# A decode step of attention and a gated MLP: the last row of weights in two pieces, a one-row store, and small loads in halves

## The chip, the cores and the metric

The kernel runs on one core of a Trainium2 chip. A time is device time in microseconds (us) of one execution, the median of several. Five engines work side by side: PE (TensorE, matmuls; its weight loads are listed as PEld), DVE (VectorE), ACT (ScalarE), POOL (GpSimd) and SP (SyncE, which here only issues transfers and waits). Data comes from HBM through 16 DMA engines that all queues share. SBUF and PSUM have 128 partitions; PSUM takes the results of PE.

## The reference

One token, D = 576. Two branches see the same x and are mixed by a gate:

```
g = sigmoid(sum(x * gate_w))
q = x @ wq                          # 32 heads of 128
k, v = last 4096 positions of the caches, 16 heads, each for 2 heads of q
a = softmax(q k^T / sqrt(128)) v @ wo          # wo: 4096 x 576
b = gelu(x @ w1 + b1) @ w2 + b2                # w1: 576 x 4608, w2: 4608 x 576
out = g * a + (1 - g) * b                      # 1 x 576, bfloat16
```

All inputs are bfloat16. About 54 MB are read once; the output has 1152 bytes.

## The kernel before

Large tensors are read in transfers of 128 partitions, all issued by SP: eight k_t and eight v_t of 2 MB each (two heads), two each of wq, w1 and wo, and w2 as four groups (NG = 4) of 1152 rows. In a group each partition holds nine whole rows of w2 (RJ = 9, 10,368 bytes). Group 2 comes in two transfers and the last group in three: rows 0 to 5, rows 6 and 7, and row 8 alone (L625 to L630). Small loads go through ACT's queue at the very start: x, gate_w and b_2, each as one row of 1152 bytes on one partition (L130 to L132). x comes a second time, spread over 64 partitions, through SP (x9, L136).

The order of work on each engine is the order written in the kernel (a manual schedule). The gate comes first: DVE multiplies x and gate_w and sums (L385), PE spreads the sum to all partitions (g_ps, L390), ACT and DVE make the sigmoid. Then, over pairs of heads, PE transposes keys (L235), ACT and DVE copy them out of PSUM (L246, L244), PE makes scores, softmax runs in blocks of four heads, and PE multiplies with the values. The MLP's first half runs between the heads. A load into a buffer waits until PE has done with what was in it.

At the end PE multiplies wo and the first three groups of w2 into the tile part, on four rows of PSUM (partitions 0, 32, 64, 96). DVE adds these to (1 - g) * b_2 (part_s, L679). Then `row_matmul` (L688) adds everything into y_ps: one row of 576 results is held as four quarters of DQ = 144 columns, on partitions 0, 32, 64 and 96 of one PSUM tile. For each of the nine rows j of the last group there are four matmuls, one a quarter. DVE casts y_ps to the SBUF tile y, all 128 partitions at once (L703), and SP stores four of its partitions, 288 bytes each, to the output (L704).

The framework puts in the waits. Its transfers take eight completion semaphores in turn. A transfer that takes a semaphore again is issued only when the one eight before it has landed. Behind the last instruction SP waits for all of them (these stand under L732, the end of the kernel), two to an instruction, in this order in the compiled program: (4th, 3rd), (5th, 2nd), (6th, 1st), (7th, DVE), (8th, ACT); then a barrier of all engines ends the program.

Of the kernel before, what the change touches and what calls it, by code (L numbers as in the profile page):

```python
# [9 lines left out]
BF16 = mybir.dt.bfloat16  # L10
# [6 lines left out]
def kernel(  # L17
# [15 lines left out]
    nc = tc.nc  # L33

    P = 128
    D = 576
# [10 lines left out]
    NQ = 4  # L47
    DQ = D // NQ

    RJ = 9  # L50
    NG = F // (P * RJ)
# [27 lines left out]
    const = ctx.enter_context(tc.tile_pool(name="const", bufs=1))  # L79
# [13 lines left out]
    w2_view = B_w2.rearrange("(g p j) n -> g p (j n)", p=P, j=RJ)  # L93
# [31 lines left out]
    x_row = const.tile([1, D], BF16, name="x_row")  # L125
    gw_row = const.tile([1, D], BF16, name="gw_row")

    b2_r = const.tile([P, D], BF16, name="b2_r")
    nc.gpsimd.memset(b2_r[:], 0.0)
    nc.scalar.dma_start(out=x_row[:], in_=A_x.rearrange("a b d -> (a b) d"))  # L130
    nc.scalar.dma_start(out=gw_row[:], in_=gate_w.rearrange("(o n) -> o n", o=1))
    nc.scalar.dma_start(out=b2_r[0:1, :], in_=B_b2.rearrange("(o n) -> o n", o=1))  # L132

    k_tiles[0] = load_k(0)
    x9 = const.tile([P // 2, NM], BF16, name="x9")
# [3 lines left out]
    for i in range(2):  # L139
# [16 lines left out]
        out=row_f[:], in_=ident_f[:, 0 : 32 * (NQ - 1) + 1 : 32], axis=AX.X, op=ALU.add  # L156
# [4 lines left out]
        out=dup[:].rearrange("k (i e) -> k i e", e=2),  # L161
        in_=ident[0 : P // 2, 0 : P // 2].rearrange("k (i e) -> k i e", e=1).to_broadcast(
            [P // 2, P // 2, 2]
        ),
    )
    par = const.tile([P, 2], FP32, name="par")
    for o in range(2):
        nc.vector.tensor_reduce(
            out=par[:, o : o + 1],
            in_=ident_f[:].rearrange("p (i o) -> p o i", o=2)[:, o, :],  # L170
# [7 lines left out]
        out=turn[:].rearrange("p j (h q) -> p j h q", h=OJ),  # L178
        in_=ident[:].rearrange("p (o q j) -> p j o q", o=1, j=OJ).to_broadcast(
            [P, OJ, OJ, P // OJ]  # L180
        ),
# [4 lines left out]
        out=m_r[:], in_=ident_f[:].rearrange("p (s r) -> p r s", r=R), axis=AX.X, op=ALU.add  # L186
# [5 lines left out]
        out=row_e[:], in_=ident_f[:].rearrange("p (a e q) -> p e a q", e=2, q=2), axis=AX.XY,  # L192
# [3 lines left out]
        out=row_e[:], in0=row_e[:], scalar1=-MASK, scalar2=MASK, op0=ALU.mult, op1=ALU.add  # L196
    )
    mask = const.tile([P, BC * P], BF16, name="mask")
    for e in range(2):
        nc.vector.tensor_copy(  # L200
            out=mask[:, e::2], in_=row_e[:, e : e + 1].to_broadcast([P, BC * P // 2])
# [4 lines left out]
        out=m_c[:], in_=ident_f[:].rearrange("p (t c r) -> p c t r", c=BC, r=R), axis=AX.XY,  # L206
# [4 lines left out]
        out=m_hl[:], in_=ident_f[:].rearrange("p (h q) -> p h q", h=OJ), axis=AX.X, op=ALU.add  # L211
# [10 lines left out]
    for dst, src in ((sel, ident), (sel_f, ident_f)):  # L222
        nc.vector.tensor_copy(
            out=dst[:].rearrange("p l (o h) -> p l o h", o=2),
            in_=src[:].rearrange("p (h l x) -> p l x h", h=2, l=2)[:, :, 0:2, :],
# [149 lines left out]
    for dst, src, s in (  # L375
# [10 lines left out]
        out=junk[:], in0=x_row[:], in1=gw_row[:], scale=1.0, scalar=0.0,  # L386
# [11 lines left out]
        out=omg[:], in0=g_t[:], scalar1=-1.0, scalar2=1.0, op0=ALU.mult, op1=ALU.add  # L398
# [7 lines left out]
    for b in range(NM * NQ):  # L406
        m, t = b // NQ, b % NQ
# [22 lines left out]
    for m in range(HB // 2):  # L430
        lo = R * (NGR - 1) + RP * m
        nc.vector.tensor_copy(  # L432
            out=qz[:, m :: HB // 2, lo : lo + RP],
            in_=qT[:, :, m, :].rearrange("p i b -> p b i"),
# [114 lines left out]
    for h in range(NU):  # L549
# [4 lines left out]
        if h == 1:  # L554

            for o in range(2):
                nc.sync.dma_start(
                    out=b1_r[o : o + 32 * (NQ - 1) + 1 : 32],
                    in_=B_b1.rearrange("(o t k n) -> o t k n", o=2, t=NQ, k=2)[o],
# [57 lines left out]
    for i in range(NOG // 2):  # L617
        t = w_pool.tile([P, WMAX], BF16, name="wo_t", tag="w")
        nc.sync.dma_start(
            out=t[:, 0 : 2 * OJ * D].rearrange("p (o n) -> p o n", o=2),  # L620
            in_=wo_view[:, 2 * i : 2 * i + 2, :],
# [2 lines left out]
    w2_t = []  # L624
    for g in range(NG):  # L625
        t = kv_pool.tile([P, NCK * Dh], BF16, name="w2_t", tag="kv")
        cut = {NG - 2: (0, 5, RJ), NG - 1: (0, 6, 8, RJ)}.get(g, (0, RJ))
        for lo, hi in zip(cut, cut[1:]):
            nc.sync.dma_start(out=t[:, lo * D : hi * D], in_=w2_view[g, :, lo * D : hi * D])
        w2_t.append(t)  # L630

    ot = const.tile([P, Hq], BF16, name="ot")
# [1 line left out]
        out=ot[:], in0=o_sb[:], scalar=g_t[:, 0:1], in1=r_sums[:], op0=ALU.mult, op1=ALU.mult  # L634
# [3 lines left out]
    for j in range(OJ):  # L638
# [3 lines left out]
        out=ow_m[:],  # L642
# [5 lines left out]
    with nc.allow_low_precision("one of the eight summands is not zero"):  # L648
        nc.vector.tensor_reduce(  # L649
            out=ow[:].rearrange("p j o -> p (j o)"), in_=ow_m[:], axis=AX.X, op=ALU.add  # L650
# [4 lines left out]
    y_ps = ps_s.tile([P, DQ], FP32, name="y_ps", tag="s")  # L655
# [12 lines left out]
    for n, four in enumerate(blocks):  # L668
# [11 lines left out]
        out=part_s[:], in0=b2_r[:].rearrange("p (k n) -> p k n", k=2), scalar=omg[:, 0:1],  # L680
# [5 lines left out]
    quarters = [slice(t * DQ, (t + 1) * DQ) for t in range(NQ)]  # L686
# [10 lines left out]
    for j in range(RJ):  # L697
# [1 line left out]
        row_matmul(  # L699
            gt[:, j, NG - 1 : NG], [row[:, q] for q in quarters], False, j == RJ - 1  # L700
        )
    y = const.tile([P, DQ], BF16, name="y")
    nc.vector.tensor_copy(out=y[:], in_=y_ps[:])  # L703
    nc.sync.dma_start(  # L704
        out=out.rearrange("a b (t n) -> (a b t) n", t=NQ), in_=y[0 : 32 * (NQ - 1) + 1 : 32, :]
    )


# [28 lines left out]
```

## Time and profile before

| what | value |
|---|---|
| median of 3 runs | 134.98 us (134.93 to 135.19) |
| the profiled execution | 134.92 us |
| its span, first to last instruction | 133.0 us |
| mean granted TensorE clock | 0.837 |
| DMA bytes, mean rate over the span | 53.79 MB, 404 GB/s |
| share of SP's DMA queue in 16 engines' time | 95.2% |
| busy: PE, DVE, ACT | 90.9, 61.3, 48.5 us |
| last matmuls (y_ps) | 127.95 to 129.93 us |
| cast of the result (y) | 129.95 to 130.26 us |
| store issued | 130.29 us |
| SP's wait for the store ends | 131.94 us |

Times within the profile count from the span's start. The page gives busy time by engine, the span in 40 slices, the DMA queues, and the chain of work that ended last, followed back from the last instruction. A group's line has busy time and mean duration, then the idle time before it and what ended it. A line of the windows gives length, then busy time and number of instructions by engine (PE, PEld, DVE, ACT, POOL), the granted clock, the DMA engines' share and GB/s. A line of the waits has total, times and longest, in us.

### The profile page before, as it was taken

What the parts mean: (1) busy time and instruction counts of PE and PEld (TensorE: products, weight loads), DVE (VectorE), ACT (ScalarE), POOL (GpSimd) and SP (SyncE); (2) the same over time, 40 slices, a digit from 0 to 9 for tenths busy, and PEclk for the clock granted to TensorE, in tenths of its full rate; (3) what the DMA queues carried; (4) which work ended last, traced back from release to release, by engine and by line L of the source; (5) the groups of instructions that cost most, each with busy time, mean ns of one, the idle gap of its engine ahead of it and who ended that gap; (6) DMA issues with size and microseconds to landing.
All of it is one profiled execution on the core that took longest, in us unless ns stands there. A gap on an engine that the chain in (4) does not pass through costs nothing.

```text
span 133.0 us, 2659 instructions
## 1 busy us (share of the span) xinstructions
PE 90.9 (68%) x1127; PEld 58.6 (44%) x1127; DVE 61.3 (46%) x165; ACT 48.5 (36%) x91; POOL 4.2 (3%) x11
## 2 busy tenths in 40 slices
PE   0007985299296899969076996978988648459660
PEld 0007741267174565645045654645655215135340
DVE  4964632035227665575004257564866463440020
ACT  3003750066336787757001153766584100000000
POOL 8400000000000000000000000000000000000000
PEclk9999999757999999999955559999999955555865
DMA  3999999999999999999899999999999999999960
GB/s 79 400 430 432 443 424 429 434 436 412 431 458 399 453 414 446 409 421 479 379 453 409 448 414 443 419 439 424 434 429 429 415 418 430 436 424 415 428 261 0
DMA packets 4553, 53.79 MB, mean 404 GB/s; under 512 B 563, under 2 KB 702, under 8 KB 1214
## 3 DMA queue, kind: packets, MB, share of 16 engines
q1 hardware_dynamic: 4536, 53.62, 95.2%
q8 instruction: 9, 0.15, 0.4%
q14 instruction: 2, 0.02, 0.0%
q10 hardware_dynamic: 6, 0.00, 0.0%
HBM read 53.62 MB, written 0.00 MB: 403 GB/s over the span
## 4 chain that ended last, share of the span: by engine, by line
DMA 58%; PE 28%; DVE 8%; SPq 2%; issue 2%; DVEq 0%
DMA w_t<-in_B_w_dram 41%; DMA k_t<-in_A_k_cache_dram 17%; PE tp L235 13%; PE s_ps L266 4%; PE acc L342 3%; DVE kT L244 3%; PE h_ps L454 2%; PE hT L481 2%; DVE a_s L358 2%; PE y_ps L690 1%; SPq L120 1%; SPq L102 1%; DVE ez L320 1%; DVE part_s L679 1%; DVE h_r L472 1%
## 5 line engine op out<-in xcount | busy, mean ns | idle before, releaser
L246 ACT CAST kT<-tp 128x512 bf16<-128x512 f32 x80 | 44.1, 586 | 44.2 <-PE tp L235 43.7
L244 DVE CAST kT<-tp 128x512 bf16<-128x512 f32 x48 | 33.0, 690 | 38.6 <-PE tp L235 34.1
L235 PE MATMUL tp<-ident,k_t 128*128 128x128 bf16 x512 | 45.5, 238 | 4.7 <-DMA k_t<-in_A_k_cache_dram 3.0
L235 PEld LDWEIGHTS <-k_t 128*128 128x128 bf16 x512 | 35.2, 107 | 17.4 <-issue 12.8
L342 PE MATMUL acc<-v_t,ez 128*32 128x512 bf16 x128 | 13.3, 459 | 2.2 <-DVE a_s L358 1.9
L266 PE MATMUL s_ps<-kT,qz 128*32 128x512 bf16 x128 | 13.5, 416 | 0.3 <-DVE qz L432 0.3
L454 PE MATMUL h_ps<-w_t,x 128*32 128x288 bf16 x72 | 4.0, 365 | 6.8 <-DMA w_t<-in_B_w_dram 6.8
L454 PEld LDWEIGHTS <-x 128*32 128x32 bf16 x72 | 2.8, 117 | 7.6 <-issue 7.1
L373 PE MATMUL x_ps<-x,dup 64*128 64x9 bf16 x1 | 0.2, 163 | 8.8 <-DMA x<-in_A_x_dram 8.8
L342 PEld LDWEIGHTS <-ez 128*32 128x32 bf16 x128 | 3.7, 102 | 5.5 <-issue 3.1
L266 PEld LDWEIGHTS <-qz 128*32 128x32 bf16 x128 | 3.3, 94 | 3.8 <-issue 0.8
L679 DVE SCALAR_TENSOR_TENSOR part_s<-b_r,omg,part 128x576 f32<-128x576 bf16 x1 | 0.8, 814 | 8.8 <-PE part L671 8.8
L671 PE MATMUL part<-wo_t,ow 128*1 128x288 bf16 x64 | 4.0, 443 | 1.0 <-DVE ow L649 1.0
L671 PE MATMUL part<-w_t,gt 128*1 128x288 bf16 x54 | 3.7, 364 | 1.4 <-DMA w_t<-in_B_w_dram 1.4
L358 DVE SCALAR_TENSOR_TENSOR a_s<-acc,m_c,a_s 128x128 f32<-128x128 f32 x12 | 4.2, 351 | 0.4
L307 ACT ACTIVATE pr<-ms,nb 128x512 bf16<-128x512 f32 x4 | 2.9, 722 | 4.1 <-DVE nb L304 4.1
L320 DVE COPY ez<-pT 128x64 bf16<-128x64 bf16 x32 | 3.6, 183 | 1.7 <-PE pT L315 1.5
L148 DVE CAST ident_f<-ident 128x128 f32<-128x128 bf16 x1 | 3.0, 3000 | 1.8 <-POOL ident masks.py:199 1.8
L365 PE MATMUL o_ps<-m_r,a_s 128*128 128x8 f32 x8 | 1.9, 315 | 2.8 <-DVE a_s L358 2.8
L365 PEld LDWEIGHTS o_ps<-m_r,a_s 128*128 128x128 f32 x8 | 1.6, 249 | 4.9 <-DVE a_s L358 2.5
L671 PEld LDWEIGHTS <-gt 128*1 128x1 bf16 x54 | 2.2, 104 | 2.9 <-issue 2.0
L481 PE MATMUL hT<-sel_f,h_r 128*64 128x4 f32 x36 | 2.7, 264 | 1.2 <-DVE h_r L472 1.2
(82 smaller groups left out, 48.2 us busy)
## 6 DMA issues: line engine op xcount, KB each, us to landing
k_t<-in_A_k_cache_dram SPq DMA_DIRECT2D x8, 2048.0 KB, 27.5
v_t<-in_A_v_cache_dram SPq DMA_DIRECT2D x8, 2048.0 KB, 24.5
w_t<-in_B_w_dram SPq DMA_DIRECT2D x2, 2592.0 KB
wq_t<-in_A_wq_dram SPq DMA_DIRECT2D x2, 2304.0 KB, 14.4
wo_t<-in_A_wo_dram SPq DMA_DIRECT2D x2, 2304.0 KB
w_t<-in_B_w_dram SPq DMA_DIRECT2D x2, 1296.0 KB, 21.6
w_t<-in_B_w_dram SPq DMA_DIRECT2D x1, 864.0 KB
w_t<-in_B_w_dram SPq DMA_DIRECT2D x1, 720.0 KB, 21.3
```

The lines of the kernel that those rows point to most:

```text
L148: nc.vector.tensor_copy(out=ident_f[:], in_=ident[:])
L235: nc.tensor.matmul(tp[:, c * P : (c + 1) * P], lhsT=k_tiles[h // 2][:, (h % 2) * NCH + i * BC + c, :], rhs=ident[:], start=True, stop=True,)
L244: nc.vector.tensor_copy(out=dst, in_=tp[:])
L246: nc.scalar.copy(out=dst, in_=tp[:])
L266: nc.tensor.matmul(s_tiles[b][32 * t : 32 * (t + 1), :], lhsT=qz[:, h // 2, lo : lo + 32], rhs=kT[h][:, i * BC * P : (i + 1) * BC * P], st ...
L320: nc.vector.tensor_copy(out=ez[:, b % 2, m, NQ * s : NQ * (s + 1), :, RP * m : RP * (m + 1)], in_=pT[:].rearrange("p c (t s r) -> p t c s ...
L342: nc.tensor.matmul(acc[b][32 * ct : 32 * ct + 4 * R, :, :], lhsT=ez[:, b % 2, ul // 2, n, :, :].rearrange("p c r -> p (c r)"), rhs=v_tiles ...
L358: nc.vector.scalar_tensor_tensor(out=a_s[:], in0=acc[b][:, c, :], scalar=m_c[:, c : c + 1], in1=a_s[:], op0=ALU.mult, op1=ALU.add,)
L365: nc.tensor.matmul(o_ps[:], lhsT=a_s[:], rhs=m_r[:], start=True, stop=True)
L454: nc.tensor.matmul(h_box[0][32 * t : 32 * (t + 1), k, 0:FB], lhsT=x2[:, m, :], rhs=w[:, off : off + FB], start=(m == 0), stop=(m == NM - 1),)
L481: nc.tensor.matmul(box[0][64 * e : 64 * (e + 1), j, :], lhsT=rows[:, j : j + RJ * 63 + 1 : RJ], rhs=sel_f[:, e, :], start=True, stop=True,)
L671: nc.tensor.matmul(part[32 * t : 32 * t + 1, k, 0:DB], lhsT=col, rhs=w[:, i * D + k * DB : i * D + (k + 1) * DB], start=(n == 0), stop=(n ...
```

## The change

Three things are changed. The last row of the last group of w2 comes in two transfers: the first three quarters (864 bytes a partition) and the last quarter (288 bytes). The result is copied quarter by quarter into one partition: ACT copies the first two quarters, DVE the last two; SP stores this one row of 1152 bytes. And x, gate_w and b_2 are each loaded in two halves of 576 bytes, so that ACT issues six transfers in place of three.

```
-    nc.scalar.dma_start(out=x_row[:], in_=A_x.rearrange("a b d -> (a b) d"))
-    nc.scalar.dma_start(out=gw_row[:], in_=gate_w.rearrange("(o n) -> o n", o=1))
-    nc.scalar.dma_start(out=b2_r[0:1, :], in_=B_b2.rearrange("(o n) -> o n", o=1))
+    for o in (slice(0, D // 2), slice(D // 2, D)):
+        nc.scalar.dma_start(out=x_row[:, o], in_=A_x.rearrange("a b d -> (a b) d")[:, o])
+    for o in (slice(0, D // 2), slice(D // 2, D)):
+        nc.scalar.dma_start(out=gw_row[:, o], in_=gate_w.rearrange("(o n) -> o n", o=1)[:, o])
+    for o in (slice(0, D // 2), slice(D // 2, D)):
+        nc.scalar.dma_start(out=b2_r[0:1, o], in_=B_b2.rearrange("(o n) -> o n", o=1)[:, o])
...
-        cut = {NG - 2: (0, 5, RJ), NG - 1: (0, 6, 8, RJ)}.get(g, (0, RJ))
-        for lo, hi in zip(cut, cut[1:]):
-            nc.sync.dma_start(out=t[:, lo * D : hi * D], in_=w2_view[g, :, lo * D : hi * D])
+        cut = {NG - 2: (0, 5 * D), NG - 1: (0, 6 * D, 8 * D, RJ * D - DQ)}.get(g, (0,))
+        for lo, hi in zip(cut, (*cut[1:], RJ * D)):
+            nc.sync.dma_start(out=t[:, lo:hi], in_=w2_view[g, :, lo:hi])
...
-    y = const.tile([P, DQ], BF16, name="y")
-    nc.vector.tensor_copy(out=y[:], in_=y_ps[:])
-    nc.sync.dma_start(
-        out=out.rearrange("a b (t n) -> (a b t) n", t=NQ), in_=y[0 : 32 * (NQ - 1) + 1 : 32, :]
-    )
+
+    y = const.tile([1, D], BF16, name="y")
+    for t in range(NQ):
+        copy = nc.scalar.copy if t < 2 else nc.vector.tensor_copy
+        copy(out=y[:, quarters[t]], in_=y_ps[32 * t : 32 * t + 1, :])
+    nc.sync.dma_start(out=out.rearrange("a b n -> (a b) n"), in_=y[:])
```

## The prediction

> **What bounds the kernel now.** I read the page's second and third parts first. For nearly the whole span the 16 DMA engines are full, and one queue, SP's, carries 53.62 of the 53.79 MB. So a load counts only where it leaves that stream dry, and everything behind the last byte counts in full. TensorE's granted clock drops to 0.5 for the end.
>
> ```profile
> PEclk9999999757999999999955559999999955555865
> DMA  3999999999999999999899999999999999999960
> ...
> q1 hardware_dynamic: 4536, 53.62, 95.2%
> ...
> q10 hardware_dynamic: 6, 0.00, 0.0%
> ```
>
> Next the end of the chain that ended last and the timeline of the last microseconds: weights arrive, matmuls, one cast on DVE, one store.
>
> ```profile
> 126.50 0.55 PE part L671 x9
> 127.05 0.02 issue
> 127.08 0.82 DVE part_s L679
> 127.90 0.04 issue
> 127.95 1.98 PE y_ps L690 x44
> 129.93 0.02 issue
> 129.95 0.31 DVE y L703
> ```
>
> ```profile
> 129.61 0.09 PEld L690 LDWEIGHTS <-gt 128*1 128x1 bf16 x3
> ...
> 130.29 0.60 SPq L704 DMA_DIRECT2D out_dram<-y  x1
> ```
>
> Then windows of a tenth of a microsecond and less (the last two columns are DMA share and GB/s). They show when the weights' stream ends (129.25 to 129.30) and when two small transfers move their bytes: the first load of x (1.6 to 1.7) and the store (131.5 to 131.6).
>
> ```profile
> 1.60:1.70 0.10, 0.00 (x0) 0.00 (x0) 0.00 (x0) 0.00 (x0) 0.10 (x1) 1.00 0.04 12
> ...
> 129.20:129.25 0.05, 0.05 (x12) 0.04 (x5) 0.00 (x0) 0.00 (x0) 0.00 (x0) 0.50 0.07 23
> 129.25:129.30 0.05, 0.05 (x12) 0.05 (x7) 0.00 (x0) 0.00 (x0) 0.00 (x0) 0.50 0.01 0
> ...
> 131.50:131.60 0.10, 0.00 (x0) 0.00 (x0) 0.00 (x0) 0.00 (x0) 0.00 (x0) 0.50 0.07 12
> ```
>
> Last, SP's waits, and the closing line's instructions on SP in the window 131.90 to 132.24:
>
> ```profile
> SPq L704 <- DVE y L703: 13.1, 1, 13.1
> SPq L704 <- DMA wo_t<-in_A_wo_dram: 5.2, 1, 5.2
> ...
> SPq L557 <- DMA k_t<-in_A_k_cache_dram: 4.0, 1, 4.0
> SPq L732 <- DMA out_dram<-y: 1.0, 1, 1.0
> ```
>
> ```profile
> L732 SPq EVENT_SEMAPHORE  x5: 28/28/28, 131.9 to 132.2; - x5
> ```
>
> The reader is to see four serial steps. (1) The last bytes land and row 8 starts at 129.61, about 0.33 behind the stream's end, though TensorE ran its earlier rows 0.12 apart and could have begun at about 129.47. (2) DVE copies from 129.95 to 130.26. (3) The store is issued at 130.29, moves its bytes 1.21 to 1.31 later, and is seen by SP at 131.94. (4) SP then still works through five closing waits, 0.065 apart, although all but the first had been met long before. The two wait lines on other DMAs show a ring: the store's issue had to wait for the second wo_t load, eight transfers earlier, and the first half of b_1 for k_t, eight earlier.
>
> **The change part by part.** The sum is made against the profiled execution, 134.92 us (span 133.0 and 1.9 around it); the median of the runs, 134.98, is 0.06 above it.
>
> *The last row in two pieces.* One transfer of 1152 bytes a partition becomes 864 and 288. SP issues one DMA more (0.33 us for such a piece), around 112 to 118, eleven us or more ahead of its bytes; the ring makes it wait for the second wo_t load, which landed at 117.1. Hidden by the queue ahead of it; were it not, its 0.33 would count. The bytes are the same, but each of the 16 engines moves 8 packets and a completion more. In the windows, one packet of 1152 bytes with its completion took 0.04 x 16 x 0.1 = 0.064 us of one engine, and four of 288 with theirs 0.07 x 16 x 0.1 / 4 = 0.028 each. A line through these gives 0.016 per packet before its bytes, completion included, so the ends are 0 and 8 x 0.016 = 0.13. I take 0.05, nearer to nothing, because a completion comes once per piece and not per packet. So 288 bytes land 0.05 later than now, and 864 bytes some 8 x 0.01 = 0.08 earlier, since 288 bytes at that slope are 0.01.
> The Trainium skill (DMA: Bandwidth & Descriptors, "How a descriptor splits into AXI transactions") says that a read starts at a 256-byte boundary and fetches the bytes ahead of its start. By that, and by the page's 32 bytes at 850 MHz, I estimate 0.08 for this step in place of 0.05, and a sum 0.03 higher. No run here shows such a packet yet.
>
> *Four copies for one.* The cast on DVE took 0.309 for 128x144; a reduction of 1x128 took 0.279 and those of 128x128 took 0.276 to 0.361, so I give one partition no discount. Eight independent copies (ez) of 0.18 took 0.88 in all, so the next starts 0.08 before the last one ends: two copies on DVE take 0.31 + 0.23 = 0.54. On ACT 512 elements took 0.586 and one element 0.171, so 144 take 0.29; two 512-element casts in a row took 1.07, 0.10 less than twice 0.586, so two take 0.48, beside DVE. ACT did nothing after 107 and delays nothing. With the third quarter free 0.08 earlier, DVE starts at 129.87, its second copy at 130.10, when the fourth quarter (130.00) is there, and it ends at 130.41 against 130.26: +0.15. Ends: +0.10 if DVE's copies overlap more, +0.28 if all four wait for the whole row (130.00 + 0.54). The store now waits for two engines; one more wait on SP costs at most 0.065, and I take 0.03, since ACT should be first.
>
> *One row stored in place of four.* The store of four rows took 1.21 to 1.31 from issue to bytes. The nearest row of the new form is the first load of x: one row of 1152 bytes, issued at 0.73, bytes in 1.6 to 1.7, so 0.87 to 0.97. The page counts six packets on ACT's queue for three such loads: one of data and one completion each. Difference 0.34 (0.24 to 0.44). Against it: that was a load on ACT's queue. SP's own first load was issued at 0.73 and moved its first bytes after 2.1, 1.4 later; if the engine and not the number of rows sets this time, the step gives nothing or costs 0.1. I take -0.34, as the form is the same; ends -0.44 and +0.1.
>
> *Where the store's semaphore stands.* The page's sixth part lists 36 transfers: 8 k_t, 8 v_t, 2 each of wq, w_1, wo and b_1, 7 of w_2, four small loads and the store. The store is the 36th and has the fourth of eight semaphores in turn. The compiled program of before lists the closing waits as (4th, 3rd), (5th, 2nd), (6th, 1st), (7th, DVE), (8th, ACT): the first one waits for the store, and four follow at 0.065. Three more small loads and one more piece make 40, so the store gets the eighth, the last wait, and the other four pass while it is in flight: -0.26. If the order does not hold, 0; it cannot cost, since the store already stands first.
>
> *Small loads in halves.* ACT issues six DMAs for three (0.21 to 0.50 each), done by about 3; its first arithmetic is at 11.09. On ACT's queue data moved at 1.6, 4.2 and 6.05, so every 1.9 once k_t streams. The second half of gate_w is the fourth, at about 7.9, landed by about 9; DVE reads it at 9.61 and then releases PE's first transposes at 10.98. Cover 0.6. If it is gone, PE starts that much later, but PE idles 6.8 for w_1 later and the loads are issued some 24 us ahead, so the end does not move. b_2 is not read before 127.08. SP's early loads move on the ring: a wq_t or k_t load may now wait for the first k_t (landed by 8.6) in place of being issued by 4. The first wq_t lands by 14.0 (the first v_t's issue waited for it), so the stream has work until about 13.6. Together 0; ends 0 and +0.9 (below).
>
> Sum: +0.15 + 0.03 - 0.34 - 0.26 = -0.42, so 134.50 on the profiled time and 134.56 on the median.
>
> **The rivals.**
> *Whole row first.* The copies are released by the row's last matmul only. In the trace DVE's cast starts 0.05 behind it, and nothing reads a part of a PSUM tile that is still being written, so the rows do not decide. The copies cost 0.28, the sum is -0.29: 134.69.
> *ACT, then DVE.* The four copies read one PSUM tile, and are put one engine after the other: 129.87 + 0.48 + 0.05 + 0.54 = 130.94, +0.68; sum +0.11, 135.09. No pair of engines reads one tile at once in the trace. The Trainium skill (PSUM — Partial Sum Buffer, "PSUM bank collisions raise a hardware error") bears on it: two engines may not use one bank in the same 32 partitions at once, reads included, but different groups of 32 may, and guarding whole banks is the simple form. The four quarters lie in four such groups; no run here shows either form yet.
> *The closing waits stay.* -0.16, 134.82.
> *The store is no quicker.* -0.08, 134.90.
> *The stream runs dry (slower).* If the second wq_t waits on the ring for the last half of b_2, sixth on ACT's queue: its bytes move at 7.9 + 2 x 2.1 = 12.1 (wq_t's rows are 18 KB against k_t's 16, so 1.9 becomes 2.1), the completion 0.65 later (as with b_2 now, 6.05 and 6.7), landed at 13.1; wq_t's bytes start 1.4 behind, at 14.5, and the engines have stood from 13.6: +0.9, sum +0.48, 135.46. It costs nothing up to a landing at 12.2 and makes the kernel slower from 12.9 on. Against it: nothing says that this load gets that semaphore, and earlier members of the ring land by 9.
>
> **How the numbers follow.** Forecast case 0.42; whole row first 0.24; ACT then DVE 0.10; closing waits stay 0.10; store no quicker 0.08; dry stream 0.06. A change under 0.2%, 0.27 us, can't be told from none here. Faster: nearly all of the first, over half of the second, some of the rest, 0.62. Slower: most of the dry stream, and some of the serial copies and of a dearer store, 0.13. Within: 0.25. The range goes from 134.3 (store -0.44, copies +0.10, and 0.1 of spread) to 135.1 (serial copies); the forecast case alone spans 134.35 to 134.75.
>
> **What would show it.** Right: the store's bytes move within 1.0 of its issue; one closing wait on SP behind its landing, not five; two copies on ACT beside two on DVE, y complete 0.15 behind the present 0.31 after row 8; the last three matmuls of row 8 in front of the fourth. Wrong: ACT's copies ending before DVE's begin; DMA share below 0.9 between 10 and 16; the stream's end later than 129.4.

## The result and the profile after

The changed kernel takes 134.73 us (median of 9 runs, 134.66 to 134.87) against 135.06 us (134.93 to 135.28) for the kernel before: a ratio of 0.9978, with a 95% interval of 0.9969 to 0.9986. So it is 0.3 us faster (0.19 to 0.42). The profiled execution of the changed kernel took 134.87 us with a span of 133.1 us. It is one of its slower ones, and only 0.05 below the profiled execution of before. Where the two profiles differ by less than 0.1 the comparison of the many runs decides, not this pair. PE's granted clock differs in the pair too: 0.5 from 123 on in the changed kernel, 1.0 from 124 to 127 and 0.5 from 127.5 on in the kernel before, so the first line below has 0.89 for the nine matmuls that took 0.55 before.

The timeline of the changed kernel's end. The columns are start, length, engine and line, tiles, number; in brackets the idle time before and what ended it.

```profile
126.48 0.89 PE L674 MATMUL part<-w_t,gt 128*1 128x288 bf16 x9 [0.53 <-DMA w_t<-in_B_w_dram]
127.41 0.81 DVE L682 SCALAR_TENSOR_TENSOR part_s<-b_r,omg,part 128x576 f32<-128x576 bf16 x1 [10.89 <-PE part L674]
...
130.03 0.56 ACT L709 CAST y<-y_ps 1x144 bf16<-1x144 f32 x2 [24.70 <-PE y_ps L693]
130.10 0.64 DVE L709 CAST y<-y_ps 1x144 bf16<-1x144 f32 x2 [1.88 <-PE y_ps L693]
130.81 0.28 SPq L710 DMA_DIRECT2D out_dram<-y  x1
```

ACT and DVE copy side by side, and y is complete at 130.74, 0.48 later than the single cast left it (130.26). The store is issued in 0.28 in place of 0.60. Windows of the changed kernel (length, busy time by engine, clock, DMA share, GB/s) show the end of the weights' stream and the store's bytes:

```profile
129.25:129.30 0.05, 0.05 (x12) 0.05 (x4) 0.00 (x0) 0.00 (x0) 0.00 (x0) 0.50 0.04 6
...
131.50:131.60 0.10, 0.00 (x0) 0.00 (x0) 0.00 (x0) 0.00 (x0) 0.00 (x0) 0.50 0.03 12
```

The stream ends where it ended before. The store's bytes move 0.7 to 0.8 behind its issue; it was 1.2 to 1.3. Copies and store together are a draw in this pair: SP sees the store's landing at 131.95, before it was 131.94. Then come SP's closing instructions, here those between 130.5 and 131.7, and then those up to 132.33:

```profile
L736 SPq EVENT_SEMAPHORE  x4: 28/28/28, 131.1 to 131.3; - x4
```

```profile
L736 SPq EVENT_SEMAPHORE  x2: 17/22/28, 131.9 to 132.2; - x2
L736 SPq DRAIN  x3: 7/7/13, 132.0 to 132.3; - x3
```

Four of the five closing waits now pass while the store is in flight, and the first drain follows the landing by 0.06: at 132.0 where it was 132.26. That gain of 0.25 does not reach the end of the span, for DVE is late in the last barrier. Its closing instructions in the changed kernel, then in the kernel before (both from 131.9 on):

```profile
L736 DVEq EVENT_SEMAPHORE  x2: 21/21/21, 132.2 to 133.0; - x2
L736 DVEq DRAIN  x1: 136/136/136, 132.7 to 132.7; - x1
```

```profile
L732 DVEq EVENT_SEMAPHORE  x2: 21/21/21, 132.5 to 133.0; - x2
L732 DVEq DRAIN  x1: 19/19/19, 132.6 to 132.6; - x1
```

Before, the drain follows DVE's wait by 0.1. In the changed kernel it follows by 0.5 and takes 136 ns in place of 19. POOL, the last of the other engines, is done at 132.54 and the barrier goes on at 132.89; before, it went on 0.04 behind POOL. So about 0.3 is lost here. No step of the prediction had this.

Last, SP's waits in the changed kernel:

```profile
SPq L120 <- DMA k_t<-in_A_k_cache_dram: 5.8, 1, 5.8
...
SPq L736 <- DMA out_dram<-y: 0.6, 1, 0.6
```

The second wq_t load now waits for the first k_t, by the ring of semaphores, and is issued at 8.5 in place of 2.7. The DMA engines stayed full.

### The profile page after: what moved, and what is told of

It reads as the page before. It is cut to its first block, busy times and chain, and to the rows that moved or that the text cites. A ratio compares the mean times of both kernels' runs of the same rounds, so it can differ in the third digit from the quotient of the medians.

```text
span 133.1 us, 2668 instructions
## 1 busy us (share of the span) xinstructions
PE 92.4 (69%) x1127; PEld 59.2 (45%) x1127; DVE 61.7 (46%) x166; ACT 49.3 (37%) x93; POOL 4.2 (3%) x11
## 4 chain that ended last, share of the span: by engine, by line
DMA 61%; PE 27%; DVE 8%; issue 1%; SPq 1%; DVEq 0%
DMA w_t<-in_B_w_dram 42%; DMA k_t<-in_A_k_cache_dram 18%; PE tp L238 13%; PE s_ps L269 4%; PE acc L345 3%; DVE kT L247 3%; PE hT L484 2%; DVE a_s L361 2%; PE y_ps L693 1%; PE h_ps L457 1%; PE part L674 1%; DVE ez L323 1%; DVE part_s L682 1%; DVE h_r L475 1%; PE o_ps L368 0%
## 5 line engine op out<-in xcount | busy, mean ns | idle before, releaser
L238 PE MATMUL tp<-ident,k_t 128*128 128x128 bf16 x512 | 47.1, 245 | 4.3 <-DMA k_t<-in_A_k_cache_dram 3.0
L238 PEld LDWEIGHTS <-k_t 128*128 128x128 bf16 x512 | 36.9, 111 | 17.6 <-issue 13.1
L269 PE MATMUL s_ps<-kT,qz 128*32 128x512 bf16 x128 | 14.2, 436 | 0.3 <-DVE qz L435 0.3
L709 ACT CAST y<-y_ps 1x144 bf16<-1x144 f32 x2 | 0.5, 268 | 24.7 <-PE y_ps L693 24.7
L674 PE MATMUL part<-w_t,gt 128*1 128x288 bf16 x54 | 4.3, 381 | 3.1 <-DMA w_t<-in_B_w_dram 3.1
L457 PE MATMUL h_ps<-w_t,x 128*32 128x288 bf16 x72 | 3.0, 295 | 4.3 <-DMA w_t<-in_B_w_dram 4.3
L457 PEld LDWEIGHTS <-x 128*32 128x32 bf16 x72 | 2.3, 96 | 4.7 <-issue 4.6
```

The lines of the kernel that those rows point to most:

```text
L238: nc.tensor.matmul(tp[:, c * P : (c + 1) * P], lhsT=k_tiles[h // 2][:, (h % 2) * NCH + i * BC + c, :], rhs=ident[:], start=True, stop=True,)
L269: nc.tensor.matmul(s_tiles[b][32 * t : 32 * (t + 1), :], lhsT=qz[:, h // 2, lo : lo + 32], rhs=kT[h][:, i * BC * P : (i + 1) * BC * P], st ...
L457: nc.tensor.matmul(h_box[0][32 * t : 32 * (t + 1), k, 0:FB], lhsT=x2[:, m, :], rhs=w[:, off : off + FB], start=(m == 0), stop=(m == NM - 1),)
L674: nc.tensor.matmul(part[32 * t : 32 * t + 1, k, 0:DB], lhsT=col, rhs=w[:, i * D + k * DB : i * D + (k + 1) * DB], start=(n == 0), stop=(n ...
```

## The experiments

The theory drawn from the profile after: the closing waits give 0.25, copies and store about 0.1 together, and the halves do nothing at the start. The rivals: the one-row store alone gives the gain; the barrier behind SP takes up what the closing waits save; the halves cost at the start. After the first runs a further theory came in, the number of DVE's instructions.

In the following, a ratio is to the kernel before on the same chip, and 0.001 is 0.135 us. "Around the span" is the time less the span of the same execution, mean over the runs; the kernel before has 1.94 to 1.97.

**Store and copies alone.** The kernel before with the changed kernel's last block:

```
-    y = const.tile([P, DQ], BF16, name="y")
-    nc.vector.tensor_copy(out=y[:], in_=y_ps[:])
...
+    y = const.tile([1, D], BF16, name="y")
+    for t in range(NQ):
+        copy = nc.scalar.copy if t < 2 else nc.vector.tensor_copy
+        copy(out=y[:, quarters[t]], in_=y_ps[32 * t : 32 * t + 1, :])
...
```

> The kernel before with only the four copies and the one-row store: 36 transfers, so the store keeps the fourth semaphore, the first closing wait. Theory (after's trace: store 0.51 quicker from issue to landing, copies 0.43 longer): 0.08 us faster than before or nothing, ratio 0.9990 to 1.0005. Rival (the one-row store is where the gain lies): 0.3 faster, ratio 0.998. The prediction's terms gave 0.03 + 0.28 - 0.34, which is also nearly nothing.

Ratio 0.9979 (0.9970 to 0.9989): 0.28 faster, as the rival had it. But its profile does not show 0.28 there. From the start of row 8's last matmul (129.54) to the store's landing (131.75) it took 2.21, against 2.31 before. The rest, about 0.2, lies around the span: 1.75.

**Small loads whole.** The changed kernel with the three loads of before:

```
-    for o in (slice(0, D // 2), slice(D // 2, D)):
-        nc.scalar.dma_start(out=x_row[:, o], in_=A_x.rearrange("a b d -> (a b) d")[:, o])
+    nc.scalar.dma_start(out=x_row[:], in_=A_x.rearrange("a b d -> (a b) d"))
...
```

> The changed kernel with x, gate_w and b_2 loaded whole: 37 transfers, the store takes the fifth semaphore, which stands in the second closing instruction, three ahead of the last. Theory (ring): 3 x 0.065 = 0.20 us slower than the changed kernel, so about 0.13 faster than before, ratio 0.9990. Rival (halves do nothing by the ring): as the changed kernel, ratio 0.9978.

Ratio 0.9966 (0.9952 to 0.9979), where both expectations had 0.9978 or more. Three closing waits came back behind the landing, as the ring says, and yet the kernel is not slower than the changed one. Something else in the changed kernel costs more than these 0.2; around the span 1.73.

**Halves with x9 split too**, to reach 40 transfers without the rest of the change, and **row 8 whole**, the changed kernel with the same filler:

```
-    nc.sync.dma_start(out=x9[:], in_=A_x.rearrange("a b (i m) -> (a b i) m", m=NM))
+    for o in (slice(0, P // 4), slice(P // 4, P // 2)):
+        nc.sync.dma_start(out=x9[o], in_=A_x.rearrange("a b (i m) -> (a b i) m", m=NM)[o])
```

> The kernel before with its small loads in halves and x9 also in two halves, so 40 transfers in all: the store takes the eighth semaphore, and nothing else of the change is made. Theory (the gain is the closing waits): 0.26 us faster than before, ratio 0.9981, with one closing wait behind the store's landing. Rival (the barrier behind SP's waits takes the gain up, or halves cost at the start): within 0.1 us of before, ratio 0.9993 to 1.0007.

> The changed kernel with row 8 in one transfer again, and x9 in two halves to keep 40 transfers and the store on the eighth semaphore. Theory (the 288-byte piece lands 0.09 later and lets DVE's second copy start no earlier, since its first copy is still running): 0 to 0.1 us faster than the changed kernel, ratio to before 0.9970 to 0.9978. Rival (the split lets three copies start earlier): 0.1 slower than the changed kernel, ratio 0.9985.

Ratios 1.0156 (1.0142 to 1.0170) and 1.0143 (1.0129 to 1.0157): both 2 us slower, which nobody expected. Windows of the second, and one line of SP's waits in it:

```profile
6.00:8.00 2.00, 0.00 (x0) 0.00 (x0) 1.93 (x10) 0.00 (x0) 0.00 (x0) 1.00 0.83 346
8.00:10.00 2.00, 0.16 (x1) 0.10 (x1) 0.62 (x6) 0.00 (x0) 0.00 (x0) 1.00 0.60 129
10.00:12.00 2.00, 1.06 (x8) 1.07 (x9) 1.03 (x6) 0.17 (x1) 0.00 (x0) 1.00 0.72 304
12.00:14.00 2.00, 1.75 (x17) 1.53 (x15) 1.08 (x4) 1.07 (x2) 0.00 (x0) 1.00 1.02 433
```

```profile
SPq L120 <- DMA k_t<-in_A_k_cache_dram: 6.0, 1, 6.0
```

The second half of x9 took the semaphore that the first wq_t load has in the changed kernel, so now the first wq_t is the one that waits for k_t. Nothing is in the queue behind k_t, and from 8 to 12 the engines move 129 and 304 GB/s where 433 is the rule: (1 - 129/433) x 2 + (1 - 304/433) x 2 = 2.0 us of stream lost, which is what the kernels lost. In the kernel before the same two windows have 406 and 415 GB/s. This is the dry stream of the prediction's slower rival, one transfer further on. The times of the two kernels say nothing on what they were made for.

**Halves alone.** The kernel before with the small loads in halves as in the changed kernel, 39 transfers:

```
-    nc.scalar.dma_start(out=x_row[:], in_=A_x.rearrange("a b d -> (a b) d"))
+    for o in (slice(0, D // 2), slice(D // 2, D)):
+        nc.scalar.dma_start(out=x_row[:, o], in_=A_x.rearrange("a b d -> (a b) d")[:, o])
...
```

> The kernel before with only the small loads in halves: 39 transfers, the store takes the seventh semaphore, the fourth closing instruction. Theory (the ring saves three closing waits, nothing is lost at the start because the first wq_t goes on the first half of x and only the second wq_t waits for k_t): 0.19 us faster than before, ratio 0.9986. Rival (the halves cost as much as the ring gives, which the kernel with whole small loads hints at by being 0.15 faster than the changed one): ratio 1.000 or above.

Ratio 0.9974 (0.9963 to 0.9985): 0.35 faster, more than the ring's 0.19. The halves cost nothing. Around the span: 1.73.

**Four-row store.** The changed kernel with the last block of before, the first diff turned round:

> The changed kernel with the cast of all partitions and the four-row store of before; 40 transfers, the store on the eighth semaphore, row 8 in two pieces. Theory (one-row store and four copies are worth 0.25 together, as they gave alone): 0.25 slower than the changed kernel, about as before, ratio 0.999 to 1.001, although four closing waits are gone. Rival (store and copies cancel, the ring gives the gain): as the changed kernel, ratio 0.998.

Ratio 0.9981 (0.9972 to 0.9990): 0.26 faster without the one-row store, the rival's side. Around the span 1.72. By now the store alone, the halves alone and all but the store had each gained what the whole change gains. The gains do not add, and each has 0.2 around the span.

**The ring by other transfers.** The changed kernel with whole small loads, and two groups of w_2 cut further to reach 40:

```
-        cut = {NG - 2: (0, 5 * D), NG - 1: (0, 6 * D, 8 * D, RJ * D - DQ)}.get(g, (0,))
+        cut = {0: (0, 5 * D), 1: (0, 3 * D, 6 * D), NG - 2: (0, 5 * D), NG - 1: (0, 6 * D, 8 * D, RJ * D - DQ)}.get(g, (0,))
```

> The changed kernel with whole small loads, and the first two groups of w_2 in two and three transfers: 40 transfers again, so the store takes the eighth semaphore, but the order at the start is that of before. Theory (ring): three closing waits fewer than with whole small loads, 0.19 us faster than that, 0.61 faster than before, ratio 0.9955. Rival (what stands behind SP's closing waits takes it up, as DVE's late last drain did in the changed kernel's profile): as with whole small loads, ratio 0.9966.

Ratio 0.9973 (0.9964 to 0.9983): 0.36 faster than before and not faster than with whole small loads (0.9966), against the theory.

**Copies in the other order.** The changed kernel with whole small loads and

```
-    for t in range(NQ):
+    for t in (1, 0, 3, 2):
         copy = nc.scalar.copy if t < 2 else nc.vector.tensor_copy
```

> The changed kernel with whole small loads and each engine's two copies in the other order, so that the later quarter's wait covers the second copy. Theory (a copy that waits starts only when the one ahead of it is done, 0.33 behind its start on DVE; one without a wait overlaps by 0.08): y complete 0.1 earlier or, as the first copy on DVE now waits for the last matmul, the same: 0 to 0.1 us faster than with whole small loads, ratio 0.9959 to 0.9966. Rival (the wait does not matter): 0.03 slower.

Ratio 0.9981 (0.9970 to 0.9993). Timelines of the two kernels with whole small loads, first in the order of the change, then in the other:

```profile
129.86 0.56 ACT L706 CAST y<-y_ps 1x144 bf16<-1x144 f32 x2 [23.47 <-PE y_ps L690]
129.93 0.64 DVE L706 CAST y<-y_ps 1x144 bf16<-1x144 f32 x2 [2.04 <-PE y_ps L690]
```

```profile
129.84 0.55 ACT L706 CAST y<-y_ps 1x144 bf16<-1x144 f32 x2 [23.39 <-PE y_ps L690]
130.01 0.62 DVE L706 CAST y<-y_ps 1x144 bf16<-1x144 f32 x2 [2.10 <-PE y_ps L690]
```

DVE takes 0.62 for its pair without a wait between them and 0.64 with one. So the wait is not what keeps the two copies from overlapping, and the theory falls. What does is open: each pair reads two different partitions of PSUM, the eight ez copies all read the same 128, and no run separates this. y is complete at 130.57 in the order of the change and at 130.63 in the other, but 0.03 of these 0.06 is row 8's last matmul, which started later (129.72 and 129.75). The intervals of the two ratios overlap, so which order is faster is not shown.

**The number of DVE's instructions.** In the compiled programs DVE has 193 instructions in the kernel before and in the halves with x9 split; these two have 1.94 to 1.97 around the span. It has 194 in every other kernel so far, with 1.71 to 1.75 around, because a second copy, or a wait for one more half, adds one. The changed kernel has both, 195, and 1.80. The number of ACT's instructions does not sort the kernels in this way: it is 115 in the halves with x9 split and in most kernels with 194 on DVE. Three kernels change DVE's number and nothing else of weight:

```
     ones_ff = const.tile([P, P], FP32, name="ones_ff")
     nc.vector.memset(ones_ff[:], 1.0)
+    spare = const.tile([P, 1], FP32, name="spare")
+    nc.vector.memset(spare[:], 0.0)
```

> The kernel before with one more instruction on DVE, a memset of 128x1 near the start that nothing uses; so DVE has 194 instructions in place of 193. Theory (code: every kernel so far with 194 had 0.2 us less around its span than those with 193, whatever else was changed): 0.2 us faster than before, ratio 0.9985, with the span as before (133.05 to 133.1) and 1.73 around it in place of 1.95. Rival (the time around the span has to do with ACT's six loads, the store or the ring): as before, ratio 0.9995 to 1.0005.

Ratio 0.9986 (0.9974 to 0.9999): an unused memset makes the kernel before 0.19 us faster. Around the span 1.72. Its DVE has the drain on time, but then a gap of 0.46 ahead of its very last wait:

```profile
L734 DVEq EVENT_SEMAPHORE  x2: 21/21/21, 132.6 to 133.2; - x2
L734 DVEq DRAIN  x1: 19/19/19, 132.7 to 132.7; - x1
```

```
     nc.vector.memset(ones_ff[:], 1.0)
+    spare = const.tile([P, 2], FP32, name="spare")
+    nc.vector.memset(spare[:, 0:1], 0.0)
+    nc.vector.memset(spare[:, 1:2], 0.0)
```

> The kernel before with two more instructions on DVE, memsets of 128x1 that nothing uses: 195, as many as in the changed kernel. Theory (code): the stall that the changed kernel's profile shows ahead of DVE's last drain but one, 0.3 us, moves into the span, and around it stand 1.80: 0 to 0.1 us faster than before, ratio 0.999 to 1.000, slower than with one more. Rival: as before, and as with one more.

Ratio 1.0010 (1.0001 to 1.0019): a second one takes it all back and more, 0.14 slower than before. The expectation had it slower than with one more, but not slower than before. Around the span 1.83. Its DVE closes as the changed kernel's does:

```profile
L735 DVEq EVENT_SEMAPHORE  x2: 21/21/21, 133.0 to 133.8; - x2
L735 DVEq DRAIN  x1: 120/120/120, 133.5 to 133.5; - x1
```

And the changed kernel with one instruction fewer on DVE:

```
     ones_ff = const.tile([P, P], FP32, name="ones_ff")
-    nc.vector.memset(ones_ff[:], 1.0)
+    nc.gpsimd.memset(ones_ff[:], 1.0)
```

> The changed kernel with the memset of ones_ff on POOL in place of DVE: 194 instructions on DVE in place of 195, all else as changed. Theory (code): 0.1 to 0.25 us faster than the changed kernel, ratio to before 0.996 to 0.997, and no late drain on DVE. Rival: as the changed kernel, 0.9978.

Ratio 0.9956 (0.9943 to 0.9968), 134.45 us: 0.59 faster than before and 0.3 faster than the changed kernel, whose interval it does not touch. It beats both kernels. Its DVE is on time again:

```profile
L736 DVEq DRAIN  x1: 19/19/19, 132.2 to 132.2; - x1
```

The traces also show where the delay stands. In all eleven profiles with 194 or 195 instructions DVE is idle for 0.46 us ahead of its 194th compiled instruction, whatever that is. With 195 the 194th is DVE's drain in the last barrier, and every engine waits for it. With 194 it is DVE's last wait, and most of the gap falls into the time in which DVE would wait anyway. With 193 there is no 194th, and a gap there would lie behind the span. From SP's first closing drain to the end of the span it takes 0.75 us with 193 (three profiles, the next experiment's among them), 0.84 with 194 (nine) and 1.04 to 1.06 with 195 (two). Together with the time around the span that makes about 0.15 less than before with 194 and 0.16 more with 195, close to the 0.19 less and 0.14 more of the runs. One load of instructions (8192 bytes, queue q14) keeps its distance to the same place: it starts 0.65 to 0.70 behind the 194th instruction, and with 193 at 1.09 to 1.11 behind the span's end. So the place in DVE's program is shown; that the load of code is what holds DVE there is not.

**The ring alone.** The kernel before, 193 instructions on DVE, with two groups of w_2 in three transfers each:

```
-        cut = {NG - 2: (0, 5, RJ), NG - 1: (0, 6, 8, RJ)}.get(g, (0, RJ))
+        cut = {0: (0, 3, 6, RJ), 1: (0, 3, 6, RJ), NG - 2: (0, 5, RJ), NG - 1: (0, 6, 8, RJ)}.get(g, (0, RJ))
```

> The kernel before with the first two groups of w_2 in three transfers each: 40 transfers, the store on the eighth semaphore, the start and the end untouched, 193 instructions on DVE. Theory (closing waits): 0.26 us faster than before, ratio 0.9981, all of it in the span, 1.95 around it. Rival (the barrier takes it up, and what halves and store seemed to give came from DVE's code alone): ratio 0.9995 to 1.0005.

Ratio 0.9996 (0.9987 to 1.0005), around the span 1.97: no gain that can be told. Yet its profile has the closing waits where the theory put them:

```profile
L732 SPq EVENT_SEMAPHORE  x4: 28/28/28, 131.0 to 131.2; - x4
```

```profile
L732 SPq EVENT_SEMAPHORE  x2: 17/22/28, 132.0 to 132.3; - x2
L732 SPq DRAIN  x2: 7/10/13, 132.1 to 132.1; - x2
```

The landing is at 131.99 and the first drain 0.08 behind it, not 0.34. So 0.25 is saved there, and by the runs as much is lost elsewhere. The likely place is the cut itself: four more transfers of 128 rows are 32 more packets on each DMA engine. In the kernel before ACT's queue moved one packet of 1152 bytes between 4.1 and 4.3 and one completion between 4.8 and 4.9 (the last column is the share of 16 engines' time):

```profile
q10 hardware_dynamic: 1, 0.00, 1.6%
```

```profile
q10 hardware_dynamic: 1, 0.00, 0.6%
```

That is 0.016 x 16 x 0.2 = 0.051 us and 0.006 x 16 x 0.1 = 0.010. The store's four packets of 288 bytes took 0.112 with their completions, so 0.018 each without. A line through 0.018 and 0.051 leaves 0.007 per packet before its bytes, and 32 x 0.007 + 4 x 0.010 is 0.26, all of the gain. This is worked out. The traces bear it out in part: the packets of SP's queue took 126.75 us of each DMA engine in this kernel and 126.70 in the other one with further cuts in w_2, against 126.30 to 126.59 in the others without the dry stream. But this profile, at 134.75, is 0.17 below that of the kernel before, and its stream ended only 0.04 later, so the loss is in the median of the runs and not in this profile. A way to 40 transfers that adds no packets to the weights' stream was not run on the kernel before.

## Why the prediction was right

The forecast was 134.56 us, 0.42 faster; measured is 0.30 to 0.33 faster, inside the range of 134.3 to 135.1. The direction and the size held, but several terms were off and partly cancelled: the copies cost more than forecast, the store gave more, and DVE's part was missing. That the sum came out so near is in part luck. By its own steps:

- *The last row in two pieces* (taken at 0.05 later for the last quarter). The trace has the last landing of row 8 at 129.57 before and 129.66 after: 0.09. By the price per packet above it is 8 x 0.007 + 0.010 = 0.07. The Trainium skill's rule on 256-byte starts (DMA: Bandwidth & Descriptors, "How a descriptor splits into AXI transactions") gave an estimate of 0.08. The pair does not tell these apart; the other profiles without a dry stream have 129.49 to 129.64 with row 8 whole (129.98 in one) and 129.60 to 129.84 with the split. The 0.08 by which the other quarters should come earlier was worth little in the profiled execution, where PE, at clock 0.5 since 123, reached row 8 at 129.67, only 0.03 ahead of the last quarter. In four other profiles with the split and the four copies (whole small loads in both orders, the further cuts, one instruction fewer) the last matmul of row 8 starts 0.16 to 0.17 behind the third, as the prediction's sign had it. Whether the split pays by itself was not settled: no run has it alone, and the kernel that should have told fell to the dry stream.
- *Four copies for one* (+0.15, y 0.1 to 0.28 later). Here the size failed. From the start of the last matmul to a complete y it took 0.64 before and 1.04 after, 0.40 more. Two copies on DVE take 0.64, not 0.54: the overlap read from the eight ez copies does not hold for these. The rest of the 0.40 is the head start that the changed kernel's profile lacks: in the four profiles that have it, y is complete 0.80 to 0.88 behind the start of the last matmul, 0.16 to 0.24 more than before. One partition indeed has no discount (0.301 to 0.309 against 0.309). ACT's pair took 0.56, not 0.48.
- *ACT and DVE at once.* The two ran side by side on one PSUM tile (ACT from 130.03 to 130.59, DVE from 130.10 to 130.74), so the serial rival fell. The Trainium skill's finer rule (PSUM — Partial Sum Buffer, "PSUM bank collisions raise a hardware error") agrees: different groups of 32 partitions may be used at once. The whole-row rival fell too, though this profile cannot show it: with whole small loads the first copies start at 129.86 and 129.93, while the last matmul of row 8, which starts at 129.72 and takes 0.28, is still running.
- *One row stored in place of four* (-0.34, ends -0.44 and +0.1). Measured from issue to landing: 1.64 before, 1.13 after, -0.51, beyond the end that I gave. The row taken, a load on ACT's queue, had the form right and the size low.
- *Where the store's semaphore stands* (-0.26). Right: 0.25 in the trace of the kernels with 40 transfers, 0.19 with 39.
- *Small loads in halves* (0). Right: alone they cost nothing. The ring moved the second wq_t, but behind k_t (issued at 8.5) and not behind the last half of b_2 as the slower rival had it, and the first wq_t covered it. How near this was to the slower rival, the two kernels with x9 split show: one transfer more and it is 2 us.
- *Missing: what a further instruction on DVE does.* The sum had no term for it. Two more cost the kernel before 0.14; one more gains 0.19. The changed kernel gets the bad one.

The terms as measured: copies and store -0.12 (0.40 less 0.51), closing waits -0.25, DVE's instructions +0.14 make -0.23, against -0.30 (-0.42 to -0.19). The last quarter's 0.09 is not in this sum. With 194 on DVE they make -0.12 - 0.25 - 0.19 = -0.56, against -0.59 measured. They also give the halves alone (-0.19 - 0.19 = -0.38, measured -0.35), the store alone (-0.12 - 0.19 = -0.31, measured -0.28), and the kernel with two groups cut further (-0.56 + 24 x 0.007 + 3 x 0.010 = -0.36, measured -0.36). The whole small loads, with one closing wait saved, should have -0.12 - 0.07 - 0.19 = -0.38 in both orders, and have -0.46 and -0.26. One kernel they miss: the four-row store should have -0.25 - 0.19 = -0.44, and has -0.26 (-0.38 to -0.14). The split's 0.07 to 0.09, which it pays without the one-row store, would be half of that gap; the rest stays open. With DVE's count as a part, the parts add to within about 0.1 in seven kernels and to within 0.2 in the eighth. That is as far as the test goes: the -0.12 is from one profile, and the intervals of the runs are 0.2 to 0.4 wide, so the closing waits' 0.25 is shown in the traces, but by the runs only as a part of such sums.

## What to carry to other kernels

Below half a microsecond, the end of this kernel is a sum of things outside its arithmetic: which of the closing waits is the store's, how many rows the store has, and where an engine's instruction stream ends. Before a small gain is put down to an edit, compare span and time around it, and run the edit's side effect alone: here an unused memset gave two thirds of what the whole change gave. With a ring of completion semaphores, one transfer more near the start shifts who waits for whom; look up which load then waits for a large one, and whether anything is left in the queue meanwhile.

## What the runs showed of the hardware

- One more instruction on DVE, with no use, moved the time by -0.19 us (interval -0.35 to -0.01), two by +0.14 (0.01 to 0.26). DVE is idle for 0.46 us ahead of its 194th compiled instruction in every profile that has one: with 195 that delays the drain in the last barrier by 0.4, with 194 only DVE's last wait, and the time around the span is 1.72 in place of 1.95. That the fetching of DVE's code causes it is argued, not shown. The Trainium skill (Runtime: NRT & Kernel Launch, "Instruction fetch mechanics") has the code fetched in blocks of 256 instructions and takes the crossing of a block's end as mostly hidden. The 0.46 us here are not hidden; whether a block ends there no run shows.
- A one-row store of 1152 bytes landed 1.13 behind its issue, a four-row store of the same bytes 1.64, the same in every profile to 0.01; the store's issue itself took 0.27 to 0.28 against 0.60.
- Two DVE copies of 1x144 from PSUM follow each other 0.32 to 0.33 apart, with a wait between them or without, while the eight ez copies of before follow 0.10 apart at 0.18 each. Why is not shown.
- When the first wq_t had to wait for the first k_t to land, and nothing else was queued behind k_t, the stream ran dry: 2.0 us of DMA time, and both kernels were 2 us slower.
